# An attention-plus-hard-swish kernel: the first load moved to SyncE, the small token group moved last, half of a weight cast moved into a transfer

## The chip, the cores and the metric

The kernel runs on one core of one Trainium2 chip. The metric is the device time of one execution in microseconds (us); lower is better. Engines are named as in the profile: PE is TensorE's matmuls, PEld its weight loads, DVE is VectorE, ACT is ScalarE, POOL is GpSimd, SP is SyncE. A "q" after a name (SPq) is the engine's instruction queue, here mostly the issuing of DMAs.

## The reference: what is computed

The input x has 4 batches of 12480 tokens of 128 values, in float32. `inducing` has 32 rows of 128. For each batch, with scale = 1/sqrt(128):

```python
h   = softmax(scale * inducing @ x.T) @ x     # 32 x 128: every inducing row attends to all tokens
y   = softmax(scale * x @ h.T) @ h            # 12480 x 128: every token attends to the 32 rows of h
g   = y @ w_in                                # 128 -> 2048
out = (g * clip(g + 3, 0, 6) / 6) @ w_out     # hard swish, 2048 -> 128
```

Nothing of the second line can start before the first has seen all tokens of the batch. The kernel uses that y is a weighted mean of the 32 rows of h. With small values the clip is not active, and the whole of the last two lines becomes a linear and a quadratic form in the 32 weights; its coefficients are computed once for each batch from h, w_in and w_out. Checks at the end of the run send the work to a slow general path if an assumption fails; here it is not taken.

## The kernel before, in words

**Tiling.** The tokens of a batch are cut into six groups of 2048 (128 partitions times 16 tokens, 1 MB each) and a last small group of 192 tokens (48 partitions times 4, 96 KB): `groups`, lines 60 to 68. NF = 6 is the small group's index.

**Stages.** Four stages matter.

1. `a_first` (lines 340 to 433) is the first sum over tokens, for batch 0 alone; nothing runs beside it. It goes over `pieces`: half groups of 8 tokens for each partition, and the small group as one piece of 4. A piece is cast to bf16 (line 359: a piece that begins a group is halved between ACT and DVE, the others go to ACT whole), transposed by PE (line 369), copied out of PSUM to `xT` (line 371), multiplied with the inducing rows (line 378), put through Exp on ACT (line 385), and the float32r x is added with these weights into `hnd` by PE (line 392). DVE sums the weights themselves (`dacc`, `dlast`, lines 402 to 411), and POOL folds `dacc` in four adds (line 415). The loop at lines 420 to 433 sets the order by hand: in round k it transposes piece k+1, takes the weights of piece k, casts piece k+3, and adds piece k-1. Every engine executes its own instructions in that order.
2. `c_first` (lines 627 to 693) makes the coefficients of batch 0. It ends the sum (`c_den`, `c_HT`), casts w_in and w_out to bf16 on ACT (`cast_w`, line 637, four casts of four blocks each), and goes through 16 blocks of the hidden layer: `c_sq` squares a block (line 579 on ACT, every fourth on DVE, lines 576 and 577), `c_G` (line 510) feeds `c_hs` (lines 520, 522), `c_C` (line 588) adds the squared block times `w_out_b[:, jc, :]` into `cp`, and `c_L` (line 540) makes the linear part. The order is again written by hand; the first pieces of the second stage (`b_base`, line 783; `b_r`; `b_spread`, a DMA by SP, line 763) stand in between.
3. The main loop (lines 905 to 953) goes over the 100 chunks of 512 tokens of all batches, and fills in the first sum and the coefficients of the next batch.
4. The output is stored from the `os` tiles.

**Loads.** All loads of x and the weights are issued by POOL, because their destinations are float32r tiles and the source is float32. POOL issues in program order: x group 0 as two halves, the small group, the groups 1 to 5 (groups 1, 4, 5 as halves), some constants, then w_in (line 160) and w_out (line 161). After that it loads groups 0 and 1 of batch 1 as soon as the buffers of the first groups are free. The further groups are `held` until the first four spreads of the second stage have landed (`load_held`, line 132: a copy named `seen`, then the loads). SP issues the load of the inducing rows (line 106) as its first DMA, and then nothing until the spreads. PE needs the inducing rows in line 181, which stands behind 4 warming matmuls and ahead of 8 more, and the first transposes stand behind these.

**Buffers the change touches.** The `os` pool has two buffers; group 5 of batch 0 is loaded into one of them (line 117), since the five `xr` buffers hold groups 0 to 4. The pool `xb` of bf16 pieces has two buffers.

Of the kernel before, what the change touches and what calls it, by code (L numbers as in the profile page):

```python
# [9 lines left out]
FP32 = mybir.dt.float32  # L10
# [14 lines left out]
TG = 16  # L25
SL = 4
# [14 lines left out]
def kernel(  # L41
# [8 lines left out]
    nc = tc.nc  # L50
    P = nc.NUM_PARTITIONS
# [29 lines left out]
    with ExitStack() as es:  # L81
# [21 lines left out]


        I_sb = const.tile([M, C], FP32, name="I_sb")
        nc.sync.dma_start(I_sb[:, :], inducing[:, :])

        xs, xbs = {}, {}

        def load_x(b, g, cuts=(0, TG)):  # L110
            t0, p, n = groups[g]
            src = x[b, t0 : t0 + p * n, :].rearrange("(p i) c -> p i c", i=n)
            if n < TG:
                t = xlast.tile([P, n, C], FP32R, name="xl")
            elif b == 0 and g == XBUF:

                t = osp.tile([P, TG, C], FP32R, name="x5", tag="os")
            else:
                t = xin.tile([P, TG, C], FP32R, name="xr")
            for lo, hi in zip(cuts, cuts[1:]):  # L120
                lo, hi = min(lo, n), min(hi, n)
                nc.gpsimd.dma_start(t[:p, lo:hi, :], src[:, lo:hi, :])
            xs[(b, g)] = t

        load_x(0, 0, (0, 8, 16))

        held = []
        NF = NGR - 1 if rest else NGR
# [211 lines left out]
        def a_first():  # L340

            st = S[0]
            pieces = [(g, h, h + 8) for g in range(XBUF + 1) for h in (0, 8)]
            pieces.insert(2, (NF, 0, SL))
            last = len(pieces) - 1
            a1s = {}

            def cast(k):
                g, lo, hi = pieces[k]
                p = groups[g][1]  # L350
                if lo == 0:
                    xbs[(0, g)] = xbin.tile([P, TG, C], BF16, name="xb")
                xb, xf = xbs[(0, g)], xs[(0, g)]
                if hi - lo == 8 and (lo == 0 or k == last):
                    cuts = [(nc.scalar.copy, lo, lo + 4), (nc.vector.tensor_copy, lo + 4, hi)]
                else:
                    cuts = [(nc.scalar.copy, lo, hi)]
                for eng, i, j in cuts:
                    eng(xb[:p, i:j, :], xf[:p, i:j, :].bitcast(FP32))

            def transpose(k):
                g, lo, hi = pieces[k]
                t0, p, n = groups[g]
                step = 4 if k == last else 8
                for i in range(lo, hi, step):
                    j = min(i + step, hi)
                    pt = side_bank(0, [P, 1024], BF16, "pt")
                    for q in range(i, j):
                        nc.tensor.transpose(pt[:, (q - i) * p : (q - i + 1) * p], xbs[(0, g)][:p, q, :], ident_b[:p, :p])
                    eng = nc.scalar.copy if k == last and i > lo else nc.vector.tensor_copy  # L370
                    eng(st["xT"][:, t0 + i * p : t0 + j * p], pt[:, : (j - i) * p])

            def weights(k):
                g, lo, hi = pieces[k]
                t0, p, n = groups[g]
                s1 = side_bank(0, [P, 512], FP32, "s1")
                for q in range(lo, hi):
                    nc.tensor.matmul(
                        s1[:p, (q - lo) * M : (q - lo + 1) * M],
                        lhsT=st["xT"][:, t0 + q * p : t0 + (q + 1) * p],  # L380
                        rhs=I_T[:, :],
                    )
                w = (hi - lo) * M
                a1 = a1p.tile([P, TG * M], FP32R, name="a1")
                nc.scalar.activation(a1[:p, :w], s1[:p, :w], ACT.Exp, scale=scale)
                a1s[k] = a1

            def add(k):
                g, lo, hi = pieces[k]
                p, w, a1 = groups[g][1], (hi - lo) * M, a1s[k]  # L390
                for q in range(lo, hi):
                    nc.tensor.matmul(
                        st["hnd"][:M, :C],
                        lhsT=a1[:p, (q - lo) * M : (q - lo + 1) * M],
                        rhs=xs[(0, g)][:p, q, :],
                        start=(k == 0 and q == lo),
                        stop=(k == last and q == hi - 1),
                    )
                f = a1[:p, :w].bitcast(FP32)
                d = st["dacc"][:p, lo * M : hi * M]  # L400
                if g == 0:
                    nc.vector.tensor_copy(d, f)
                elif k == last - 3:
                    st["dlast"] = cst.tile([P, 8 * M], FP32, name="dlast")
                    nc.vector.tensor_copy(st["dlast"][:, :], f)
                elif k > last - 3:
                    nc.vector.tensor_add(st["dlast"][:, :], st["dlast"][:, :], f)
                    if k == last:
                        c_red(0, st["dlast"][:, :], P, 8)
                else:  # L410
                    nc.vector.tensor_add(d, d, f)
                if k == last - 4:
                    d = st["dacc"]
                    for h in (8, 4, 2, 1):
                        nc.gpsimd.tensor_add(d[:, : h * M], d[:, : h * M], d[:, h * M : 2 * h * M])
                    st.setdefault("dred", []).append(d[:, :M])
                if hi == groups[g][2]:
                    load_next(0, g)

            for k in range(3):  # L420
                cast(k)
            transpose(0)
            for k in range(last + 1):
                if k < last:
                    transpose(k + 1)
                weights(k)
                if k + 3 <= last:
                    cast(k + 3)
                if k:
                    add(k - 1)  # L430
                if k == 3:
                    half_rows()
            add(last)


        def c_red(b, src, p, n):
            st = S[b]
            st["reds"] = st.get("reds", -1) + 1
            dred = cst.tile([P, M], FP32, name=f"dred{st['reds']}")
            nc.vector.tensor_reduce(  # L440
                dred[:p, :], src.rearrange("p (s m) -> p m s", m=M), axis=AX.X, op=ALU.add
            )
            st.setdefault("dred", []).append(dred[:p, :])
# [183 lines left out]
        def c_first():  # L627

            warm(2)
            nc.scalar.copy(w_in_b[:, : F // 2], w_in_r[:, : F // 2].bitcast(FP32))  # L630
            c_den(0)
            nc.scalar.copy(w_in_b[:, F // 2 :], w_in_r[:, F // 2 :].bitcast(FP32))
            c_HT(0)
            warm(2)

            def cast_w(i, j):
                nc.scalar.copy(w_out_b[:, i:j, :], w_out_r[:, i:j, :].bitcast(FP32))

            cast_w(0, 4)
            c_G(0, 0, 6)  # L640
            sq = lambda *jbs: [c_sq(0, jb) for jb in jbs]
            cs = lambda *jcs: [c_C(0, jc) for jc in jcs]

            sg = lambda jb: (c_sq(0, jb), c_G(0, jb + 6, jb + 7))
            sg(0)
            sg(1)
            sg(2)
            cast_w(4, 8)
            b_pack(0, 0)
            b_e(0, 0)  # L650
            for c in range(4):
                b_spread(0, c)
            load_held(3)
            for jb in range(3, 7):
                sg(jb)
                cs(jb - 3)
            cast_w(8, 12)
            sg(7)
            b_f(0, 0)
            cs(4)  # L660
            sg(8)
            b_base(0, 0, 0)
            cs(5)
            sg(9)
            c_hs(0)
            b_base(0, 0, 1)
            cs(6)
            cast_w(12, 16)
            sq(10)
            cs(7)  # L670
            sq(11)
            b_r(0, 0)
            cs(8)
            sq(12)
            cs(9)
            sq(13)
            cs(10)
            b_base(0, 1, 0)
            sq(14)
            cs(11)  # L680
            sq(15)
            cs(12)
            c_L(0, 0)
            c_L(0, 1)
            b_base(0, 1, 1)
            a_cast(1, 0, ((nc.scalar.copy, 0, 2), (nc.scalar.copy, 2, 4)))
            b_prod(0, 0)
            c_BD(0)
            cs(13, 14, 15)
            c_tail(0)  # L690
            b_pack(0, 1)
            b_e(0, 1)
            c_max(0)
# [423 lines left out]
```

## Time and profile before

| what | value |
|---|---|
| median of 6 runs | 312.92 us (312.0 to 314.01) |
| the profiled execution's own time | 313.12 us |
| its span in the trace | 311.3 us |
| TensorE clock granted, mean | 0.996 of full speed |
| busy: PE, PEld, DVE, ACT, POOL | 96%, 75%, 76%, 75%, 11% of the span |
| HBM read, written | 27.67 MB, 25.56 MB |
| by the chain that ended last: PE, ACT, DMA, DVE | 72%, 11%, 7%, 5% of the span |
| end of the first sum's last matmuls (line 392) | 25.3 us |
| w_out on the chip | 27.86 us |
| first matmul of the main loop (line 800) | 40.8 us |

The span runs from the first to the last instruction; 1.8 us of the execution lie outside it. The chain that ended last is followed back from the last instruction, at each step to what released it. It names one releaser for each step, so a stage where two engines are nearly even is shown as the one that came last. A row of the timeline reads: start, duration, engine, line, operation, output and inputs with shapes, and in brackets how long the engine was idle before it and what ended that.

### The profile page before, as it was taken

To read this page: it belongs to the slowest core of one execution; us is meant where nothing else is said; L and a number is where in the kernel's file an instruction comes from. 1 tells how busy PE (TensorE), PEld (TensorE's weight loads), DVE (VectorE), ACT (ScalarE), POOL (GpSimd) and SP (SyncE) were. 2 spreads that over 40 slices of the span, in tenths; PEclk is the share of its full clock that TensorE was granted. 3 is DMA by queue.
4 is the path that set the end of the run, shared out by engine and by line. 5 is a ranking of instruction groups with operands and counts; after the bars stand their busy time and mean duration, and the time that the engine had idled before them with its cause. 6 is when DMAs were issued, how large, how long until landed. Compare 5 with 4: busy or idle time off the path is not lost.

```text
span 311.3 us, 9606 instructions
## 1 busy us (share of the span) xinstructions
PE 298.3 (96%) x3923; PEld 233.2 (75%) x3929; DVE 235.7 (76%) x543; ACT 231.9 (75%) x425; POOL 35.4 (11%) x82
## 2 busy tenths in 40 slices
PE   6899899999999999999999999999999999999992
PEld 2787678887676878888767877888867786777781
DVE  2687797977883868878796668787888487888882
ACT  3778999886589678886679849888658945777760
POOL 7611301011100010101100000100000001000000
PEclk9999999999999999999999999999999999999998
DMA  6999497988963452899975525555255335476672
GB/s 214 400 397 352 100 372 224 312 310 254 357 228 99 137 177 65 295 304 316 324 216 188 176 53 170 183 187 170 53 187 167 138 96 187 155 232 210 214 251 100
DMA packets 25089, 66.69 MB, mean 214 GB/s; under 512 B 3168, under 2 KB 17536, under 8 KB 19408
## 3 DMA queue, kind: packets, MB, share of 16 engines
q0 software_dynamic: 9232, 46.83, 43.6%
q1 hardware_dynamic: 15808, 19.19, 22.7%
q8 instruction: 32, 0.52, 0.6%
q14 instruction: 17, 0.14, 0.1%
HBM read 27.67 MB, written 25.56 MB: 171 GB/s over the span
## 4 chain that ended last, share of the span: by engine, by line
PE 72%; ACT 11%; DMA 7%; DVE 5%; issue 2%; POOL 1%; ACTq 0%; DVEq 0%; POOLq 0%
PE op L816 27%; PE bp L776 11%; PE op L800 7%; PE hnd L290 6%; ACT sq L579 6%; DMA w_out_r<-in_moe_w_out_dram 5%; PE pt L268 5%; PE cp L588 4%; PE s L276 2%; PE pp L747 2%; ACT TF L783 2%; DMA xr<-in_x_dram 2%; PE ep L703 2%; PE sp L717 1%; PE dpm L568 1%
## 5 line engine op out<-in xcount | busy, mean ns | idle before, releaser
L783 ACT ACTIVATE TF<-bp 128x512 bf16<-128x512 f32 (+1 forms) x200 | 117.2, 599 | 38.7 <-PE rp L736 21.0
L816 PE MATMUL op<-Cq,TF 128*128 128x128 bf16 (+1 forms) x800 | 109.2, 223 | 0.0
L816 PE MATMUL op<-Cq,TD 128*128 128x128 bf16 (+1 forms) x800 | 105.9, 219 | 0.0
L832 DVE TENSOR_TENSOR os<-op,r_all 128x512 f32<-128x512 f32 (+1 forms) x100 | 68.5, 685 | 18.9 <-PE op L816 17.6
L816 PEld LDWEIGHTS <-TF 128*128 128x128 bf16 (+1 forms) x800 | 50.5, 98 | 33.6 <-issue 24.7
L776 PE MATMUL bp<-xT,W 128*128 128x512 bf16 (+1 forms) x197 | 74.0, 376 | 0.1
L792 DVE TENSOR_TENSOR TD<-TF,d 128x1024 bf16<-128x1024 bf16 (+1 forms) x100 | 66.9, 669 | 1.1 <-DMA d<-dk 0.5
L816 PEld LDWEIGHTS <-TD 128*128 128x128 bf16 (+1 forms) x800 | 61.4, 98 | 0.6
L800 PE MATMUL op<-BD,nf 128*128 128x512 f32 (+1 forms) x100 | 53.3, 533 | 0.5 <-DVE os L832 0.4
L579 ACT ACTIVATE sq<-dpm 128x512 bf16<-128x512 f32 x60 | 35.2, 641 | 4.1 <-PE gp L510 1.9
L259 ACT CAST xb<-xr 128x1024 bf16<-128x1024 f32 x36 | 37.6, 1055 | 0.0
L737 DVE RECIPROCAL r_all<-rp 128x4 f32<-128x4 f32 (+1 forms) x100 | 17.8, 178 | 24.3 <-PE rp L736 23.9
L736 PE MATMUL rp<-one,nf 128*128 128x4 f32 (+1 forms) x100 | 34.5, 345 | 0.4
L269 DVE COPY xT<-pt 128x1024 bf16<-128x1024 bf16 (+1 forms) x42 | 25.8, 618 | 8.1 <-PE pt L268 7.6
L844 POOL DMA_DIRECT2D out_dram<-os x21 | 11.3, 537 | 142.7 <-DVE os L832 136.0
L290 PE MATMUL hnd<-xr,a 128*32 128x128 f32 x288 | 24.2, 226 | 0.0
L754 ACT ACTIVATE dk<-pp 128x512 bf16<-128x512 f32 (+1 forms) x28 | 15.7, 560 | 10.4 <-PE pp L747 10.4
L268 PE MATMUL pt<-ident_b,xb 128*128 128x128 bf16 x300 | 23.3, 218 | 0.0
L776 PEld LDWEIGHTS <-W 128*128 128x128 bf16 x200 | 19.5, 97 | 5.0 <-issue 3.4
L588 PE MATMUL cp<-w_out_b,sq 128*128 128x128 bf16 x256 | 22.7, 220 | 0.5 <-ACT sq L579 0.5
L568 PE MATMUL dpm<-dH,w_in_b 128*128 128x512 bf16 x62 | 22.7, 381 | 0.0
L510 PE MATMUL gp<-HTr,w_in_r 128*128 128x32 f32 x64 | 21.3, 358 | 0.3 <-ACT HTr L488 0.3
(127 smaller groups left out, 405.5 us busy)
## 6 DMA issues: line engine op xcount, KB each, us to landing
xr<-in_x_dram POOLq DMA_DIRECT2D x20, 1024.0 KB, 8.5
out_dram<-os POOLq DMA_DIRECT2D x18, 1024.0 KB, 4.4
d<-dk SPq DMA_DIRECT2D x96, 128.0 KB, 3.9
out_dram<-os SPq DMA_DIRECT2D x5, 1024.0 KB, 4.1
xr<-in_x_dram POOLq DMA_DIRECT2D x6, 512.0 KB, 5.4
x<-in_x_dram POOLq DMA_DIRECT2D x2, 512.0 KB, 13.5
w_in_r<-in_moe_w_in_dram POOLq DMA_DIRECT2D x1, 1024.0 KB, 13.5
w_out_r<-in_moe_w_out_dram POOLq DMA_DIRECT2D x1, 1024.0 KB, 16.6
```

Of the source, the lines that this page charges most:

```text
L259: eng(xb[:p, lo:hi, :], xs[(b, g)][:p, lo:hi, :].bitcast(FP32))
L268: nc.tensor.transpose(pt[:, (i - lo) * p : (i - lo + 1) * p], xb[:p, i, :], ident_b[:p, :p])
L290: nc.tensor.matmul(st["hnd"][:M, :C], lhsT=a1[:p, i * M : (i + 1) * M], rhs=xs[(b, g)][:p, i, :], start=(g == 0 and i == 0), stop=(g == NG ...
L579: nc.scalar.activation(sq[:, :], dpm[:, :], ACT.Square)
L588: nc.tensor.matmul(st["cp"][:, k * C : (k + 1) * C], lhsT=sq[:, k * P : (k + 1) * P], rhs=w_out_b[:, jc, :], start=(jc == 0 and k == 0), s ...
L736: nc.tensor.matmul(rp[:p, :SL], lhsT=nf[:, j * p : (j + 1) * p], rhs=one4[:, :])
L776: nc.tensor.matmul(bp[:, :w], lhsT=st["W"][:, k].rearrange("p m i -> p (m i)"), rhs=st["xT"][:, c0 : c0 + w],)
L783: nc.scalar.activation(st[("x", c)][:, k, :w], bp[:, :w], ACT.Exp, scale=scale)
L792: nc.vector.tensor_mul(u[:, :, :w], t[:, :, :w], d[:, :w].unsqueeze(1).to_broadcast([P, 2, w]))
L800: nc.tensor.matmul(op[:p, :], lhsT=st[("nf", g)][:, j * p : (j + 1) * p], rhs=st["BD"][:, :], start=True, stop=False, skip_group_check=True,)
L816: nc.tensor.matmul(op[:p, s * C : (s + 1) * C], lhsT=T[k][:, s * p : (s + 1) * p], rhs=st["Cq"][:, k, :], start=False, stop=(s == SL - 1 a ...
L832: nc.vector.tensor_mul(ot[:p, j * SL : (j + 1) * SL, :], op[:p, :].rearrange("p (s c) -> p s c", c=C), r_all[:p, b, c, :].unsqueeze(2).to_ ...
```

## The change

Three things are changed.

- **First half of group 0.** Its 512 KB are loaded by SP, as float32, into a buffer of the `os` pool (`x0`). ACT and DVE cast the bf16 piece from there, and DVE copies `x0` into the float32r tile that the later matmuls read. SP's load of the inducing rows stands behind it now.
- **Small group.** In batch 0 it is the last piece and no longer the third. The special handling of the last large piece moves with it (`last - 1`), and the closing of the weight sums is adapted; the load of batch 1's small group is issued fourth of the held loads and not first.
- **Cast of w_out.** Blocks 8 to 15 of `w_out_b` are written by a POOL DMA from `w_out_r`, and two of ACT's four casts go. On POOL it stands behind the folding of `dacc` and ahead of `seen`, and it waits for w_out to have landed.

```diff
         I_sb = const.tile([M, C], FP32, name="I_sb")
-        nc.sync.dma_start(I_sb[:, :], inducing[:, :])
...
             for lo, hi in zip(cuts, cuts[1:]):
                 lo, hi = min(lo, n), min(hi, n)
-                nc.gpsimd.dma_start(t[:p, lo:hi, :], src[:, lo:hi, :])
+                if (b, g, lo) == (0, 0, 0):
+
+                    x0 = osp.tile([P, TG, C], FP32, name="x0", tag="os")
+                    nc.sync.dma_start(x0[:, lo:hi, :], src[:, lo:hi, :])
+                    xs["x0"] = x0
+                else:
+                    nc.gpsimd.dma_start(t[:p, lo:hi, :], src[:, lo:hi, :])
             xs[(b, g)] = t
 
         load_x(0, 0, (0, 8, 16))
+        nc.sync.dma_start(I_sb[:, :], inducing[:, :])
...
-            pieces.insert(2, (NF, 0, SL))
+            pieces.append((NF, 0, SL))
             last = len(pieces) - 1
...
-                if hi - lo == 8 and (lo == 0 or k == last):
+                if hi - lo == 8 and (lo == 0 or k == last - 1):
...
-                    eng(xb[:p, i:j, :], xf[:p, i:j, :].bitcast(FP32))
+                    eng(xb[:p, i:j, :], xs["x0"][:, i:j, :] if k == 0 else xf[:p, i:j, :].bitcast(FP32))
+                if k == 0:
+                    nc.vector.tensor_copy(xf[:, lo:hi, :], xs["x0"][:, lo:hi, :])
...
-                step = 4 if k == last else 8
+                step = 4 if k == last - 1 else 8
...
-                    eng = nc.scalar.copy if k == last and i > lo else nc.vector.tensor_copy
+                    eng = nc.scalar.copy if k == last - 1 and i > lo else nc.vector.tensor_copy
...
+                elif k < last - 3:
+                    nc.vector.tensor_add(d, d, f)
                 elif k == last - 3:
                     st["dlast"] = cst.tile([P, 8 * M], FP32, name="dlast")
                     nc.vector.tensor_copy(st["dlast"][:, :], f)
-                elif k > last - 3:
-                    nc.vector.tensor_add(st["dlast"][:, :], st["dlast"][:, :], f)
-                    if k == last:
-                        c_red(0, st["dlast"][:, :], P, 8)
                 else:
-                    nc.vector.tensor_add(d, d, f)
+                    nc.vector.tensor_add(st["dlast"][:p, :w], st["dlast"][:p, :w], f)
...
+                if k == last:
+                    c_red(0, st["dlast"][:, :], P, 8)
...
             nc.scalar.copy(w_in_b[:, F // 2 :], w_in_r[:, F // 2 :].bitcast(FP32))
+
+            nc.gpsimd.dma_start(w_out_b[:, FB // 2 :, :], w_out_r[:, FB // 2 :, :].bitcast(FP32))
             c_HT(0)
...
-            cast_w(8, 12)
             sg(7)
...
-            cast_w(12, 16)
             sq(10)
```

## The prediction

> **What bounds the kernel now.** I read the chain of waits first: 72% of it is PE, and from the main loop's start (40.8 us) no step of it is a DMA. All three edits lie before 41 us, so the question is how much earlier the main loop starts; its PE chain then carries the shift to the end one for one. The chain up to 30 us (start, duration, what):
>
> ```profile
> 1.28 0.50 POOL xr L122
> 1.78 0.20 issue
> 1.98 4.94 DMA xr<-in_x_dram
> ...
> 11.31 16.55 DMA w_out_r<-in_moe_w_out_dram
> 27.86 0.02 issue
> 27.89 0.62 ACT w_out_b L637
> 28.50 0.01 issue
> 28.52 1.11 ACT sq L579 x2
> 29.63 0.51 ACT w_out_b L637
> ```
>
> The reader is to see a stage paced by loads until 27.86, then one paced by ACT. Next, busy time by stretch, where the last two columns are the DMA share and GB/s:
>
> ```profile
> 1.00:2.00 1.00, 0.79 (x2) 0.28 (x3) 0.15 (x1) 1.00 (x1) 0.72 (x2) 1.00 0.06 15
> 2.00:2.50 0.50, 0.50 (x3) 0.15 (x1) 0.00 (x0) 0.04 (x1) 0.50 (x1) 1.00 0.01 2
> 2.50:3.00 0.50, 0.50 (x2) 0.00 (x0) 0.00 (x0) 0.00 (x0) 0.42 (x3) 1.00 0.37 123
> 3.00:3.50 0.50, 0.44 (x3) 0.28 (x3) 0.23 (x1) 0.00 (x0) 0.50 (x2) 1.00 0.86 270
> ```
>
> The DMA engines are idle until about 2.7 but for 16 KB of inducing rows, which SP issued at 0.76; from 3.5 to 30 their share stays about 1 or more. Third, the timeline of ACT and PE:
>
> ```profile
> 12.41 0.62 ACT L359 CAST xb<-xr 128x512 bf16<-128x512 f32 x1 [1.07 <-DMA xr<-in_x_dram]
> 14.90 0.62 ACT L359 CAST xb<-xr 128x512 bf16<-128x512 f32 x1 [0.17 <-DMA xr<-in_x_dram]
> 17.80 0.62 ACT L359 CAST xb<-xr 128x512 bf16<-128x512 f32 x1 [0.39 <-DMA xr<-in_x_dram]
> ...
> 34.86 0.70 ACT L637 CAST w_out_b<-w_out_r 128x512 bf16<-128x512 f32 x1
> ```
>
> Every later group of x is waited for, so an earlier load stream is an earlier sum.
>
> **Edit 1, first half by SP.** The stream's start is what moves. POOL's first load is issued at 1.28 and moves bytes from about 2.7; SP's first DMA is issued at 0.76 and its 15 KB move between 1 and 2, say from 1.85. From then on the engines are never idle in either kernel, and the bytes are the same, so everything behind should land 2.7 - 1.85 = 0.85 us earlier; I take 0.8. Bounds: 0, if the early bytes only interleave with POOL's, and 1.07, the wait at 12.41, beyond which compute is late instead.
>
> The Trainium skill speaks against this: "DMA: Bandwidth & Descriptors", section "Issuing engines are not separate DMA queues", says that all issuers share the same 16 DMA engines and that issuing from several saves only sequencer time. By that alone the gain here would be one POOL issue, 0.50 us in the chain above, and the sum below would be 0.3 us worse. I stay with 0.8, because the engines in the rows above stand idle.
>
> What it adds: the copy x0 to float32r on DVE. DVE copies 128x256 in 0.284 us and 128x512 in 0.397 (lines 402, 299), so 128x1024 is about 0.62; at the rate of a 128x512 tensor-tensor (0.69) it would be 1.2. DVE waits 1.85 us for x here, and the float32r half is not read before 9.66. Behind it the DVE queue holds the cast of group 1's first half, and behind that the PSUM copy of piece 0 (before at 6.88). Group 1 has landed by 9.17 at the latest; from the bytes moved I estimate 8.6, now 7.8. So the PSUM copy runs at 8.3 to 9.0, and the first weights matmul at about 9.1 in place of 8.49. The inducing rows, now behind 512 KB on SP, land near 5 (estimate: SP's 1 MB stores land in 4.1 us, 256 KB in 2.7, and half the bandwidth is POOL's). PE waits for them, then runs 8 warming matmuls (2.68 us), so the first transposes are at 8.0 and not 6.22. Both delays fit together rather than add, and end at ACT being ready for group 2 at about 11.4; it lands at 12.41 - 0.8 = 11.6. Cost 0. Without that cover, each us that the rows land beyond 5.3 costs up to one us at 11.6, of which the later waits give most back: compute needs 7.4 us from there to group 5, the loads 7.97.
>
> **Edit 2, small group last.** Early on it takes 0.61 + 0.27 us from ACT, in a stretch that ends in the 1.07 us wait: gain 0. At the end it costs. Behind the last large piece ACT has an Exp of 0.27 (queued 0.2) more, and ahead of it a cast of 0.61 (queued 0.57): 0.78. ACT's idle there is 0.27 before the PSUM copy at 23.16 and 0.38 before HTr at 26.96, together 0.65, so HTr is 0.13 later. On DVE the reduction at 25.14 starts 0.1 to 0.15 later. POOL's folding of the sums (2.18 us, 22.50 to 24.68) follows a half group that now comes one place later, ends near 25.6 before the shift, and meets its matmul at 25.57. Cost 0.15; bounds 0 and 0.6, if POOL's folding is late. Moving batch 1's small load behind three others on POOL costs nothing: it is needed a batch's sum later.
>
> **Edit 3, half of the cast.** Two ACT casts go, at 32.43 and 34.86; in the chain each takes 0.50. But PE is nearly even with ACT here:
>
> ```profile
> 31.67 0.40 PE L588 MATMUL cp<-w_out_b,sq 128*128 128x128 bf16 x4 [0.31 <-ACT sq L579]
> ...
> 35.28 0.40 PE L588 MATMUL cp<-w_out_b,sq 128*128 128x128 bf16 x4
> 35.52 0.38 PE L568 MATMUL dpm<-dH,w_in_b 128*128 128x512 bf16 x1
> 36.11 0.40 PE L588 MATMUL cp<-w_out_b,sq 128*128 128x128 bf16 x4 [0.21 <-ACT sq L579]
> ```
>
> From 31.67 to 35.52 PE starts something every 0.22 us with no wait on ACT. So the first cast's 0.50 only gives ACT slack. The second ends as a wait: cp at 36.11 could start at 35.52 + 0.22 = 35.74. That is 0.37 gained, and what stood there is gone. Next late is PE itself: the linear part would start at 37.04 in place of 37.41; its input from DVE ends at 36.55, so DVE does not bind. Bounds: 0 and the 1.00 of the naive chain.
>
> The transfer must have landed when block 8 is multiplied, at 34.78 before and 34.1 after (0.65 of shift). POOL issues it when w_out has landed, about 27.1, with the 1 MB load of batch 1's group 1 ahead in the queue, which ends near 29.7 by the shift (the GB/s fall at 30.5 now). For 512 KB read at the 420 GB/s of these stretches I add 1.3 us, and about 1 us to landing: 32. Cover is 2 us. The trace holds no casting transfer to bf16; the nearest rows are the spreads, also from SBUF to SBUF, 2.7 to 8.5 us to landing, that is 29.8 to 35.6. On POOL only `seen` is behind it, which waits until 36.43 for a spread anyway. The spreads on SP share the engines with 0.5 MB more, but the first is needed at 38.8.
>
> **Sum.** -(0.8 - 0.15) - 0.37 = -1.02 us. Against the profiled execution: 313.12 - 1.02 = 312.10. The median lies 0.2 lower, so I forecast 312.92 - 1.02 = **311.9**. w_out, the other condition at 27.89, lands 0.8 earlier, while the first square is due 0.65 earlier, so it does not bind.
>
> **Rivals**, on the median.
> - *The stream is not earlier* (edit 1 gives 0 to 0.2): +0.15 - 0.37 - 0.1 = -0.3, 312.6. For it: all 16 engines are shared, and the first loads run at only 260 GB/s with a share of 1. Against it: the idle share before 2.7.
> - *ACT, not PE, paces 31 to 36*: both casts count, -0.65 - 1.00, 311.3. For it: the chain names ACT throughout. Against it: the PE rows above.
> - *The casting transfer is late* (slower): PE is in order, so each us after 34.1 at block 8 costs one us of the whole run; it eats the gain at 34.1 + 1.0 = 35.1. At the 8.5 us of the slowest spread it is 1.5 late: 313.4. At 9.6 us, the median landing of the 1 MB loads up to 50 us, it is 2.6 late: 314.5. For it: it queues behind a backlog. Against it: that backlog is 1 MB, and x itself is loaded into float32r by POOL at 400 GB/s.
> - *The change does not do what it says*: x0 lands no earlier than 5.5 and the inducing rows after 6. That is the first rival with up to 0.5 lost again.
>
> **How the numbers follow.** 0.3% is 0.94 us, about what a measurement of this kernel can tell from no change, so the bound is 311.98. Forecast case (311.5 to 312.4) 0.55, of which 0.35 lies below the bound; stream not earlier 0.13; ACT paces 0.10; late transfer 0.22, of which 0.04 is mild enough (landing before about 36.0) to stay within the bound. Faster 0.35 + 0.10 = 0.45; same 0.20 + 0.13 + 0.04 = 0.37; slower 0.18. The range, 311.0 to 313.7, takes in the second rival and the milder late transfer, and leaves out the heavier one.
>
> **What would show it.** Right: bytes moving from 1.9 at over 200 GB/s; group 2 cast at 11.5 to 11.8; w_out landing near 27.1; first square at 27.7 to 28.0; no PE wait at block 8; the linear part near 36.4. Wrong: a DMA as releaser at block 8 (line 595 of the new kernel); ACT at group 2 released by PE or DVE; the first square at 28.5 or later.

## The result and the profile after

The changed kernel is slower: median 314.85 us (313.36 to 315.62, 17 runs) against 312.69 (311.48 to 314.23, 38 runs), ratio 1.0063, 95% interval 1.0048 to 1.0077. The forecast was 311.9, range 311.0 to 313.7. The profiled execution takes 314.54 us, its span is 312.8, 1.5 us longer than before.

| event (us) | before | after | forecast shift | measured shift |
|---|---|---|---|---|
| first half of group 0 cast | 5.55 | 4.78 | -0.8 | -0.77 |
| second half of group 0 cast | 6.94 | 8.58 | | +1.64 |
| first transposes | 6.22 | 8.34 | +1.8 | +2.12 |
| group 2 cast | 12.41 | 13.95 | -0.8 | +1.54 |
| weight sums reduced (DVE) | 25.14 | 27.13 | -0.65 | +1.99 |
| first square | 28.52 | 30.52 | -0.65 | +2.00 |
| linear part | 37.41 | 39.03 | -1.02 | +1.62 |
| first matmul of the main loop | 40.77 | 42.39 | -1.02 | +1.62 |

The loss is complete at the first square; from there to the linear part 0.38 is gained. The rows for this are, of before (its first square, at 28.52, stands in the prediction) and then of after:

```profile
37.41 1.15 PE L540 MATMUL lp<-w_out_r,hs 128*32 128x128 f32 x16
```

```profile
30.52 1.11 ACT L586 ACTIVATE sq<-dpm 128x512 bf16<-128x512 f32 x2 [0.70 <-PE dpm L575]
...
39.03 1.15 PE L547 MATMUL lp<-w_out_r,hs 128*32 128x128 f32 x16
```

In two steps the reduction becomes 1.99 late: 1.54 when group 2 is cast, and 0.45 more between there and the reduction.

**The loads.** Busy time by stretch, first two lines of before, then after; as in the prediction the columns are PE, PEld, DVE, ACT, POOL (with counts), the granted clock, the DMA share, and last GB/s:

```profile
5.00:6.00 1.00, 1.00 (x5) 0.29 (x3) 0.43 (x1) 0.45 (x1) 1.00 (x3) 1.00 1.10 406
6.00:7.00 1.00, 0.70 (x9) 0.45 (x8) 0.12 (x1) 0.23 (x2) 0.78 (x2) 1.00 1.21 356
```

```profile
1.00:2.00 1.00, 0.79 (x2) 0.28 (x3) 0.15 (x1) 1.00 (x1) 0.71 (x2) 1.00 0.10 25
2.00:2.50 0.50, 0.50 (x3) 0.15 (x1) 0.00 (x0) 0.03 (x1) 0.42 (x2) 1.00 0.70 238
2.50:3.00 0.50, 0.50 (x2) 0.00 (x0) 0.23 (x1) 0.00 (x0) 0.50 (x2) 1.00 1.07 336
3.00:3.50 0.50, 0.10 (x1) 0.00 (x0) 0.00 (x0) 0.00 (x0) 0.50 (x2) 1.00 0.84 207
...
5.00:6.00 1.00, 0.93 (x3) 0.45 (x4) 0.61 (x3) 0.40 (x1) 1.00 (x3) 1.00 0.70 184
6.00:7.00 1.00, 1.00 (x4) 0.34 (x3) 0.59 (x1) 0.00 (x0) 0.72 (x1) 1.00 0.76 145
```

Bytes do move earlier: 238 GB/s from 2.0, where before had 2. But from 5 to 7 the rate is 184 and 145, where before had 406 and 356, and the DMA share of 0.70 to 0.76 says that the engines are partly idle. (From 3.0 to 5 it is already lower: 207, 195 and 236 against 270, 262 and 291.) They do not lack orders. By 4.66 POOL has issued 0.5 MB (second half), 96 KB, and three loads with 2 MB, SP 0.5 MB, some 3.2 MB in all; by 5.0 about 0.75 MB have moved (the GB/s summed from 1 to 5). ACT's rows show what this does (in brackets its idle time and what ended it):

```profile
8.58 1.04 ACT L364 CAST xb<-xr 128x1024 bf16<-128x1024 f32 x1 [3.18 <-DMA xr<-in_x_dram]
10.12 0.62 ACT L364 CAST xb<-xr 128x512 bf16<-128x512 f32 x1 [0.50 <-DMA xr<-in_x_dram]
...
13.95 0.62 ACT L364 CAST xb<-xr 128x512 bf16<-128x512 f32 x1 [0.74 <-DMA xr<-in_x_dram]
...
16.36 0.62 ACT L364 CAST xb<-xr 128x512 bf16<-128x512 f32 x1
```

Three casts wait for loads, the last of them group 2's. Group 3, at 16.36, shows no wait any more, though its load had landed only at 16.34; behind it no cast waits, and compute sets the pace. In before groups 3 and 4 waited again (0.17 and 0.39), and every load from group 2 to the last half of group 5 was cast within 0.03 us of its landing (the last landed at 21.63 and was cast at 21.65): there the loads set the pace to the end.

**The end of the sum.** The chain of waits of after (start, duration, what) no longer runs through w_out's load, as before's does, but through PE:

```profile
3.05 1.61 POOL xr L126 x3
4.66 11.68 DMA xr<-in_x_dram
...
24.64 0.49 PE hnd L399 x8
25.13 0.20 PE pt L376 x4
25.33 0.30 PE s L385 x8
25.63 0.49 PE hnd L399 x8
26.12 0.20 PE s L385 x4
26.33 0.96 PE hnd L399 x12
```

The small piece is `pt` x4, `s` x4 and the last 4 of `hnd` x12. Its steps stand between those of the large pieces, in PE's order, and each has another engine behind it. The timeline shows its last steps, with the last large piece's transposes at 23.78:

```profile
23.78 0.62 PE L376 MATMUL pt<-ident_b,xb 128*128 128x128 bf16 x8
...
26.36 0.27 ACT L392 ACTIVATE a<-s 48x128 fp32r<-48x128 f32 x1 [0.31 <-PE s L385]
...
26.86 0.43 PE L399 MATMUL hnd<-xl,a 48*32 48x128 f32 x4
27.13 0.60 DVE L447 TENSOR_REDUCE dred<-dlast 128x32 f32<-128x256 f32 x1
```

ACT's Exp waited for PE, and PE's last add stands behind the add of the piece before. From the last large piece's transposes to the reduction it is 3.35 us (23.78 to 27.13), before 2.63 (22.51 to 25.14):

```profile
22.51 0.62 PE L369 MATMUL pt<-ident_b,xb 128*128 128x128 bf16 x8
...
25.14 0.60 DVE L440 TENSOR_REDUCE dred<-dlast 128x32 f32<-128x256 f32 x1
```

**The cast by a transfer.** POOL's issue, and PE around block 8:

```profile
28.43 0.58 POOL L641 DMA_DIRECT2D w_out_b<-w_out_r  x1 [1.60 <-DMA w_out_r<-in_moe_w_out_dram]
...
36.54 0.38 PE L575 MATMUL dpm<-dH,w_in_b 128*128 128x512 bf16 x1
36.57 0.35 PE L743 MATMUL rp<-one,nf 128*128 128x4 f32 x1
36.79 0.40 PE L595 MATMUL cp<-w_out_b,sq 128*128 128x128 bf16 x4
```

The transfer lands 5.8 us after its issue, near 34.2. Block 8 is multiplied at 36.79 with no wait in brackets, 2.6 us after.

### The profile page after: what moved, and what is told of

The parts are those of the page before. It is cut to its first block, busy times and chain, and to the rows that moved or that the text cites. A ratio compares the mean times of both kernels' runs of the same rounds, so it can differ in the third digit from the quotient of the medians.

```text
span 312.8 us, 9607 instructions
## 1 busy us (share of the span) xinstructions
PE 297.8 (95%) x3924; PEld 233.2 (75%) x3929; DVE 236.6 (76%) x544; ACT 230.8 (74%) x423; POOL 36.0 (12%) x82
## 4 chain that ended last, share of the span: by engine, by line
PE 76%; ACT 9%; DVE 6%; DMA 4%; issue 2%; POOL 1%; ACTq 0%; DVEq 0%; POOLq 0%
PE op L823 27%; PE bp L783 12%; PE op L807 7%; PE hnd L295 6%; ACT sq L586 5%; PE cp L595 5%; PE pt L273 5%; DMA xr<-in_x_dram 4%; PE s L281 2%; PE pp L754 2%; ACT TF L790 2%; PE dpm L575 2%; PE sp L724 2%; PE ep L710 2%; PE hnd L399 1%
```

## The experiments

The theory after the result: early SP traffic stalls POOL's stream of loads from 5 to 7, and the small group costs a whole round of the pipeline at the end. Rivals: for the stall, DVE's copies or the inducing rows behind `x0`; for the end, only ACT's spare time. One table of all runs follows: GB/s in the stretches 5 to 6 and 6 to 7, the cast of group 2, the time from there to the reduction, the first square, the start of the main loop (one profile each, us); then the median and the timed ratio to before, which is worked out over all comparable runs and need not be the quotient of the medians. The medians of before beside them are 312.75 (e1 to e4), 312.82 (e5 to e7), 312.43 (e8 to e11) and 313.01 (e12 to e15).

| run | GB/s 5-7 | group 2 | to reduction | first square | main loop | median | ratio [95%] |
|---|---|---|---|---|---|---|---|
| before | 406, 356 | 12.41 | 12.73 | 28.52 | 40.77 | 312.69 | 1 |
| after | 184, 145 | 13.95 | 13.18 | 30.52 | 42.39 | 314.85 | 1.0063 [1.0048, 1.0077] |
| e1_edit1 | 266, 219 | 13.20 | 12.03 | 28.62 | 40.88 | 313.19 | 1.0016 [0.9995, 1.0037] |
| e2_edit2 | 412, 359 | 12.93 | 13.30 | 29.82 | 42.77 | 314.27 | 1.0040 [1.0021, 1.0059] |
| e3_edit3 | 418, 352 | 12.55 | 12.78 | 28.71 | 40.57 | 312.20 | 0.9996 [0.9978, 1.0015] |
| e4_edit23 | 397, 356 | 13.10 | 13.17 | 29.66 | 41.53 | 313.23 | 1.0019 [1.0000, 1.0038] |
| e5_actcopy | 186, 156 | 13.75 | 13.21 | 30.35 | 42.22 | 315.30 | 1.0082 [1.0052, 1.0113] |
| e6_poolx0 | 404, 363 | 12.79 | 13.54 | 29.70 | 41.57 | 314.03 | 1.0032 [1.0009, 1.0056] |
| e7_isbfirst | 381, 340 | 12.55 | 13.19 | 29.13 | 40.99 | 313.27 | 1.0013 [0.9989, 1.0037] |
| e8_isbact | 213, 195 | 13.73 | 13.19 | 30.30 | 42.17 | 314.57 | 1.0076 [1.0063, 1.0089] |
| e9_best | 358, 322 | 12.87 | 12.00 | 28.25 | 40.12 | 312.93 | 1.0003 [0.9988, 1.0018] |
| e10_small10 | 432, 350 | 12.67 | 13.77 | 29.83 | 42.09 | 313.59 | 1.0052 [1.0035, 1.0069] |
| e11_warm | 160, 215 | 13.54 | 13.18 | 30.11 | 41.97 | 313.63 | 1.0045 [1.0031, 1.0059] |
| e12_actx0 | 166, 234 | 13.49 | 13.19 | 30.07 | 41.93 | 314.66 | 1.0050 [1.0021, 1.0079] |
| e13_late | 406, 344 | 12.83 | 13.44 | 29.67 | 41.52 | 315.22 | 1.0076 [1.0043, 1.0108] |
| e14_both | 381, 311 | 13.38 | 12.97 | 29.74 | 41.60 | 313.75 | 1.0034 [1.0006, 1.0061] |
| e15_again | 176, 170 | 13.60 | 13.18 | 30.17 | 42.03 | 314.22 | one time |

How far to trust it: single times of one kernel spread over 2 to 3 us, and the rest of the span behind the main loop's start varies from 269.3 to 271.4 us between these profiles. So an effect below a microsecond is read from the events ahead of the main loop, and the timed ratio says whether it reaches the end.

### One part at a time

`e1_edit1` is before with the new first half alone; `e2_edit2` with the small group last alone; `e3_edit3` with the transfer alone; `e4_edit23` is the changed kernel without the new first half. The edits are the parts of the diff above, for example of e3:

```diff
+            nc.gpsimd.dma_start(w_out_b[:, FB // 2 :, :], w_out_r[:, FB // 2 :, :].bitcast(FP32))
...
-            cast_w(8, 12)
...
-            cast_w(12, 16)
```

> The kernel before with the first edit alone (first half of group 0 by SP, copied to float32r on DVE). Theory P: DVE's two float32 copies of x0 (5.5 to 6.6 in the changed kernel) keep POOL from writing DMA descriptors, so the load stream stalls there. Theory R: SP's 512 KB and POOL's loads share the 16 engines badly, so POOL's stream runs slower from its start, whatever DVE does. Both expect the same here: under 200 GB/s at 5.5 to 7, group 2 landing at 13.5 to 14, and 1.0 to 1.4 us slower than before. If the loss came from the moved small group instead, this kernel would be no slower than before.

> The kernel before with the second edit alone (small group as the last piece). Loads as before: group 2 cast at 12.4, last large piece transposed at 22.5. Theory: PE's own order at the end of the first sum, not ACT, prices the move: 0.7 us from there to the reduction, so 0.5 to 0.7 slower than before. The prediction's step (ACT slack) expects 0.15 slower.

> The kernel before with the third edit alone (blocks 8 to 15 of w_out cast by a POOL transfer). Theory (the prediction's step): PE is nearly even with ACT there, so 0.37 faster, linear part at 37.0 and not 37.4. Rival, the chain taken at its word: 1.0 faster, linear part at 36.4. Rival, late transfer: PE waits for a DMA at block 8 and the kernel is slower.

> The changed kernel with the first edit undone. If the three edits add up: 0.6 (small group) - 0.37 (cast) = 0.1 to 0.3 slower than before, and 1.2 to 1.6 faster than the changed kernel. If the small group last only costs because the loads are late, this is 0.2 to 0.4 faster than before.

e3 does what was forecast between the first square and the linear part, 8.51 us against 8.89. e2 is the surprise: the small group alone costs 0.4% (0.7 to 1.8 us by the interval). Its profile shows more than that edit. From 28 to 32 the granted clock was 0.66 there and 1.00 in before, as these lines show (before, then e2):

```profile
28.00:32.00 4.00, 3.68 (x40) 2.57 (x40) 3.18 (x8) 3.99 (x9) 0.00 (x0) 1.00 0.73 278
```

```profile
28.00:32.00 4.00, 3.67 (x23) 2.14 (x22) 3.17 (x8) 2.67 (x7) 0.00 (x0) 0.66 0.83 311
```

e2 took 3.59 us from the reduction to the first square (before 3.38), and 9.60 from there to the linear part (before 8.89). So 0.9 of the 2.00 us by which its main loop starts late go with the clock, and 1.09 at the reduction are left: 0.52 because group 2 landed later in this profile, 0.57 on the way from there (the clock was 0.83 from 10 to 20, too). Whether the edit has a part in the later landing is not shown; among the profiles without the slow loads, group 2 is cast anywhere from 12.41 to 13.10 where it waits for its load.

In e1 the slow stretch is there:

```profile
5.00:6.00 1.00, 1.00 (x4) 0.39 (x5) 0.74 (x3) 0.27 (x1) 1.00 (x3) 1.00 1.30 266
6.00:7.00 1.00, 1.00 (x4) 0.44 (x3) 0.40 (x1) 0.00 (x0) 0.52 (x1) 1.00 1.02 219
```

The rate is low, though here the DMA share (1.30, 1.02) does not show idle engines as in after. Group 2 is 0.79 late, yet the reduction is only 0.09 late (25.23): with the small group in third place the pieces run from group 2 to the reduction in 12.03 where before took 12.73, because before stood waiting for its loads. That gap of 0.7 takes the delay in. What is left is the loads' own delay at the end, which is small: by group 4's second half they had caught up, as ACT's casts of before and then of e1 show (first the second half of group 4, then that of group 5):

```profile
19.10 1.04 ACT L359 CAST xb<-xr 128x1024 bf16<-128x1024 f32 x1
...
21.65 0.62 ACT L359 CAST xb<-x 128x512 bf16<-128x512 f32 x1
```

```profile
19.19 1.05 ACT L365 CAST xb<-xr 128x1024 bf16<-128x1024 f32 x1
...
21.74 0.62 ACT L365 CAST xb<-x 128x512 bf16<-128x512 f32 x1
```

In e4, where the small group is last, the same way takes 13.17, and 13.18 or 13.19 in after, e7, e8, e11, e12 and e15, with group 2 cast anywhere from 12.55 to 13.95: no slack is left, and each delay of group 2 goes through whole. (e2, e6 and e13, at 13.30 to 13.54, take longer; e6 and e13 wait once more for a load, of group 5 and of group 4.) The clock is not behind this: in e4, e7, e8 and e12 it was 0.57 on average from 10 to 14, in after, e11 and e15 1.00, and the way is the same. So adding the late loads to e4 should show in full, and it does: from e4 to after group 2 moves by 0.85 and the main loop's start by 0.86; with e15, the same kernel as after, it is 0.50 and 0.50. The price of one edit depends on the other.

### Does a copy on DVE, or the row load behind it, stall POOL's stream?

`e5_actcopy`: the changed kernel with both passes over `x0` on ACT, so that DVE makes no copy of it.

```diff
-                if hi - lo == 8 and (lo == 0 or k == last - 1):
+                if hi - lo == 8 and k and (lo == 0 or k == last - 1):
...
-                    nc.vector.tensor_copy(xf[:, lo:hi, :], xs["x0"][:, lo:hi, :])
+                    nc.scalar.copy(xf[:, lo:hi, :], xs["x0"][:, lo:hi, :])
```

> The changed kernel, with both passes over x0 (the bf16 cast and the copy to float32r) on ACT, none on DVE. ACT is idle from 5.4 to 8.6 there. Theory P (DVE's float32 copies keep POOL from writing descriptors): the load rate at 5.5 to 7 is over 300 GB/s, the second half of group 0 lands near 7.3 and not 8.6, group 2 near 12.5, and the kernel is 1.0 to 1.4 faster than the changed one. Theory R (SP's and POOL's loads share the engines badly): the rate at 5.5 to 7 stays under 200 GB/s and the time within 0.3 of the changed kernel.

Busy time by stretch in e5:

```profile
5.00:6.00 1.00, 0.93 (x3) 0.46 (x4) 0.19 (x1) 1.00 (x2) 1.00 (x3) 1.00 0.64 186
6.00:7.00 1.00, 1.00 (x4) 0.34 (x3) 0.00 (x0) 0.77 (x1) 0.27 (x1) 1.00 0.79 156
```

DVE is nearly idle and the stall is as before: the copies are not its cause. They do cost POOL something else: its six issues from 3.04 take 3.68 us in after, where the copy runs from 5.92 to 6.59 beside the last of them, and 3.23 in e5; in e11, where the copy starts at 6.09 with the issues nearly done, they take 3.26. The Trainium skill describes this in "SBUF — State Buffer", section "SBUF: two separate sides": while DVE runs a float32 copy in a two-port mode, GpSimd can't write the descriptors of its DMAs. The 0.45 us of issue agree with it; the idle engines from 5 to 7 are not explained by it.

`e6_poolx0` lets POOL load `x0` (the copies stay); `e7_isbfirst` puts the inducing rows ahead of `x0` on SP, so that `x0` is issued at 1.20 and not at 0.76.

```diff
-                    nc.sync.dma_start(x0[:, lo:hi, :], src[:, lo:hi, :])
+                    nc.gpsimd.dma_start(x0[:, lo:hi, :], src[:, lo:hi, :])
```

```diff
         I_sb = const.tile([M, C], FP32, name="I_sb")
+        nc.sync.dma_start(I_sb[:, :], inducing[:, :])
...
-        nc.sync.dma_start(I_sb[:, :], inducing[:, :])
```

> The changed kernel, with x0 loaded by POOL and not by SP, still as float32 and still copied by DVE. Theory P: the stream stalls while DVE copies, at about 6 to 7.5, and group 2 lands at 13 or later. Theory R: no stall, loads as in the kernel before, group 2 at 12.4.

> The changed kernel with SP's load of the inducing rows ahead of x0 again. PE then warms at 3.2 to 6 and is ready for the first piece at 6, but the second piece and the loads behind it do not come earlier. P and R both expect no gain over 0.2 over the changed kernel; a gain of 0.5 or more would mean that PE's late warm-up, and not the loads, sets the loss.

Busy time by stretch in e7:

```profile
5.00:6.00 1.00, 1.00 (x4) 0.40 (x3) 0.79 (x2) 0.62 (x1) 1.00 (x3) 1.00 1.10 381
6.00:7.00 1.00, 1.00 (x9) 0.50 (x7) 0.26 (x1) 0.33 (x1) 0.44 (x2) 1.00 1.26 340
```

Neither stalls. For e6 that was expected. For e7 it was not: the expectation gave at most 0.2 us, and the first square came 1.39 earlier than in after. Two readings were left: the rows behind `x0` do harm, or `x0` at 0.76 does. `e8_isbact` has the rows issued by ACT, `x0` alone on SP:

```diff
-        nc.sync.dma_start(I_sb[:, :], inducing[:, :])
+        nc.scalar.dma_start(I_sb[:, :], inducing[:, :])
```

> The changed kernel with the load of the inducing rows issued by ACT, so that SP issues x0 alone and as early as in the changed kernel. Theory Q (the 16 KB queued behind x0 on SP, for which PE waits until 5, goes with the stall): no stall, over 300 GB/s at 5 to 7, group 2 at 12.5 to 12.9, 1.2 to 1.6 faster than the changed kernel. Theory R2 (x0 begun at 2.0, before POOL's loads, is what disturbs POOL's stream): stall as in the changed kernel, and within 0.5 of its time.

213 and 195 GB/s, group 2 at 13.73, ratio 1.0076: nothing stands behind `x0` on SP, and the stall is there. The rows are not the cause.

### Where the small group's cost comes from

`e10_small10` is before with the small group as the eleventh piece, two places ahead of the end.

```diff
-            pieces.insert(2, (NF, 0, SL))
+            pieces.insert(10, (NF, 0, SL))
...
-                    nc.vector.tensor_add(st["dlast"][:, :], st["dlast"][:, :], f)
+                    nc.vector.tensor_add(st["dlast"][:p, :w], st["dlast"][:p, :w], f)
```

> The kernel before with the small group as the eleventh piece, ahead of the last large group, and nothing else changed. Theory T (the cost of the second edit is the small piece's own transposes, weights and adds behind the last large piece): the 0.7 us at the end go, so 0.7 or more faster than the kernel with the second edit alone, and 0 to 0.4 slower than before. If the cost is at the start (DVE held by the cast of group 1), it stays: 0.8 to 1.5 slower than before.

The tail was then as short as before (2.55 from the last transposes to the reduction), but those transposes came at 23.89, 1.38 late (group 2 had been 0.26 late); the first square was 1.31 late, ratio 1.0052. My theory that the cost lies only at the tail fell. The small piece takes a whole round of PE, ACT and DVE wherever it stands among pieces that follow each other without slack; in third place it ran in a wait for loads.

### More on the stall

`e9_best` joins what had not cost: before with the new first half (rows first) and the transfer, the small group third. `e11_warm` is the changed kernel with 10 warming matmuls for 4, so that PE is not idle from 3.1 to 5.

```diff
-        warm(4)
+        warm(10)
```

> The kernel before with the first edit, but the inducing rows ahead of x0 on SP, and with the third edit; the small group stays third. If the parts add: loads 0.3 earlier at group 2, the last transposes 0.1 to 0.5 earlier, and 0.37 from the cast: 0.4 to 0.9 faster than before. If the earlier loads are worth nothing, 0.3 faster at most.

> The changed kernel with 10 and not 4 warming matmuls ahead of the wait for the inducing rows, so that PE is busy from 1.2 to about 5 and not idle from 3.1. If PE's idleness is behind the stall, the rate at 5 to 7 rises over 300 GB/s and the kernel gains 1 us or more; if the order on SP is, the stall and the time stay within 0.5 of the changed kernel.

e9 reached the first square 0.27 and the main loop 0.65 earlier than before in its profile, but the ratio is 1.0003, so the expected 0.4 to 0.9 us are not there in the times. It is no faster than before as far as this can be measured; nor is e3. e11 kept the stall (160, 215): PE's idleness is not the cause.

`e12_actx0` has ACT issue `x0` (at 0.75) in place of SP; `e13_late` puts two loads of 16 KB ahead of it on SP, so that it is issued at 1.67; `e14_both` loads both halves of group 0 by SP (and casts and copies both); `e15_again` is the changed kernel once more.

```diff
-                    nc.sync.dma_start(x0[:, lo:hi, :], src[:, lo:hi, :])
+                    nc.scalar.dma_start(x0[:, lo:hi, :], src[:, lo:hi, :])
```

```diff
+        nc.sync.dma_start(I_sb[:, :], inducing[:, :])
+        I_two = const.tile([M, C], FP32, name="I_two")
+        nc.sync.dma_start(I_two[:, :], inducing[:, :])
...
-        nc.sync.dma_start(I_sb[:, :], inducing[:, :])
```

```diff
-                if (b, g, lo) == (0, 0, 0):
+                if (b, g) == (0, 0):
...
-                if k == 0:
+                if k < 2:
```

> The changed kernel with x0 issued by ACT as its first instruction, at about the same time, and the inducing rows alone on SP. Theory R2 (an early start of x0 ahead of POOL's loads disturbs POOL's stream, whoever issues it): stall at 5 to 7 (150 to 250 GB/s), within 0.6 of the changed kernel. If SP's queue itself is the cause: over 300 GB/s there and 1 us or more gained.

> The changed kernel with two loads of 16 KB (the inducing rows, and the same again into a spare tile) ahead of x0 on SP, so that x0 is issued at about 1.6 and not 0.76. Theory R2: no stall at 5 to 7, as in the kernel with one load ahead; x0 lands near 5.6, group 2 at 12.5 to 13, 0.8 to 1.5 faster than the changed kernel. If one load ahead was no cure but a chance, the stall is back.

> The changed kernel with both halves of group 0 by SP (1 MB, both copied by DVE), so that POOL begins with the small group and group 1. If the stall comes from two queues reading the two 4 KB halves of the same 8 KB rows, it goes: over 300 GB/s at 5 to 7. If it comes from SP's early traffic itself, it stays or lengthens, to 8 or 9.

> The changed kernel once more, for a second profile. If the stall belongs to the kernel: again under 250 GB/s at 5 to 7 and group 2 at 13.3 or later. If it was one execution's chance: over 300 GB/s and group 2 at 12.5.

Busy time by stretch in e12 and then in e14:

```profile
5.00:6.00 1.00, 1.00 (x4) 0.33 (x3) 0.73 (x2) 0.31 (x1) 1.00 (x3) 1.00 0.50 166
6.00:7.00 1.00, 1.00 (x5) 0.45 (x4) 0.00 (x0) 0.00 (x0) 0.38 (x1) 1.00 0.83 234
```

```profile
5.00:6.00 1.00, 0.00 (x0) 0.00 (x0) 0.00 (x0) 0.25 (x1) 0.92 (x2) 1.00 1.25 381
6.00:7.00 1.00, 0.57 (x2) 0.31 (x3) 0.25 (x2) 0.96 (x1) 0.14 (x1) 1.00 1.09 311
```

With ACT as the issuer the stall stays (DMA share 0.50). With both halves on SP it is gone, although `x0` starts at 0.76 there too; what e14 gains is lost again to compute (ACT not ready for group 2 until 13.38, with no wait for a load). e15 stalls like after, so it is no accident of one execution. e13 shows no stall and a main loop 0.87 earlier than after, but `x0` landed at 7.03 and not near 5.6, and the times do not bear the gain out (ratio 1.0076). Five of its eight runs had a granted clock of 0.981 to 0.987 and took 315.2 to 315.6 us; the three at 0.992 to 0.994 took 313.0 to 314.4. e2's profile, at 0.982, shows that such a mean can hold a stretch that costs 0.9 us; whether e13's timed runs hold one there is not on record.

So seven profiles stall (after, e1, e5, e8, e11, e12, e15): in all of them `x0` is issued at about 0.76 by SP or ACT while POOL loads the other half of the same rows. Of the nine that do not, e7, e9 and e13 issue it at 1.20 or later, e6 has it on POOL, e14 has no other half on POOL, and the others have no `x0`. The median of group 2 is 13.60 in the stalled ones and 12.81 in the nine others together with before: 0.8 us. The times go the same way but for e13: of the kernels with the small group last, those that stall have ratios of 1.0045 to 1.0082, those that do not 1.0013 to 1.0040. What happens inside the DMA engines stays open. That two queues read the two halves of the same 8 KB runs of memory with an offset fits all of this, but was not tried by itself.

## Why the prediction was wrong

- **"The stream's start is what moves … everything behind should land 2.7 - 1.85 = 0.85 us earlier": this step failed**, and it is the larger one. Its premise held: bytes moved from about 2.0 at 238 GB/s and the first half was cast 0.77 earlier. The sentence "from then on the engines are never idle in either kernel" did not: the share fell to 0.70, the second half came 1.64 later and group 2 1.54 later (1.19 in e15). Of this 0.85 (0.50) is beyond e4, the same kernel with POOL loading the first half; the rest is in e4's profile too. The bound from below, 0, stood for bytes that only interleave; no row excluded a loss.
- **"Cost 0.15" for the small group: the term that was mis-sized.** It was worked out as ACT's added time less ACT's idle time. With loads as in before it costs 0.45 at the reduction (13.18 against 12.73), and where loads are not waited for 1.18 (13.18 against 12.00 in e9), since in the hand-written order the piece is a whole round of three engines in a row. The times put it at 0.7 to 1.8 us (e2), so 0.45 is too low for them. POOL's folding, which I had feared, bound nothing.
- **The two together.** The prediction noted that "compute needs 7.4 us from there to group 5, the loads 7.97": the slack that takes in a late group 2. (In after, where no load is waited for, compute needs 7.66, from 13.95 to 21.61.) Edit 2 removes that slack. Therefore e1 loses 0.11 at the main loop's start, but the same edit on top of e4 loses 0.86 (0.50 in e15). The sum at the main loop's start: e3 -0.20; from e3 to e4 +0.96; from e4 to after +0.86; in all +1.62. Of the +0.96, 0.55 is group 2 cast later in e4's profile than in e3's (13.10 and 12.55), 0.39 the longer way to the reduction. The -0.20 is edit 3's -0.38 behind a first square that was 0.19 late in that profile.
- **The rows behind `x0`: right.** They landed near 5.0 as estimated, the first transposes were at 8.34 (forecast 8.0), and group 2's cast was still released by a DMA. DVE's copy took 0.67 (forecast 0.62) and hindered no cast.
- **Edit 3: right**, in mechanism and size. 37.41 - 28.52 = 8.89 before, 8.51 after and in e3, 8.50 in e4: -0.38, forecast -0.37; PE and not ACT was next. In the times 0.38 can't be told from nothing (e3: 0.9996, 0.9978 to 1.0015). The transfer landed near 34.2 and not at 32. Measured from w_out's landing, as the prediction counted, it is later by about 1 us; the rest is the delay of the whole. Two misreadings stand behind it and partly cancel. The fall of the GB/s at 30.5 was taken for the end of the load ahead in POOL's queue, but that load landed at 32.84 in before and 33.10 in after, 5.0 us behind w_out and not 2.6; and the transfer landed 1.1 us behind that load and not 2.3. It was needed at 36.8.
- **The rivals.** None was this one. "The stream is not earlier" looked at the right place, but was priced as a lost gain. The late transfer, which held all of the 0.18 given to a slower kernel, did not occur, nor did `x0` or the rows land late (4.76 and 4.94). Of the signs named, "the first square at 28.5 or later" came true; the DMA at block 8 and the release of group 2 by PE or DVE did not.
- **The page.** By "Issuing engines are not separate DMA queues" (the Trainium skill, "DMA: Bandwidth & Descriptors") a second issuer saves only its issue time. That I stood against it on the ground of idle engines was half right: the first 0.77 us were real. But the runs differ from the page too: who issues, and when, changed what the other queue moved (184 and 145 GB/s in after, 404 and 363 in e6), a loss that this section does not name.

## What to carry to other kernels

Before pricing a moved step in a hand-ordered pipeline, find the stretch in which it now hides: a small piece costs its whole round where nothing waits, and little or nothing where everyone waits for a load; and the slack that it uses up is then missing for the next late load. When a transfer is started earlier on another queue, look at the stream behind it in the first microseconds, and not only at its own landing; idle engines are no proof that added orders are free. Price edits one on top of the other, not singly: here the new first half cost 0.10 us at the first square alone, and 0.86 on top of the small group last (0.51 in the second profile of the same kernel).

## What the hardware showed that was not expected

- A 512 KB load issued at 0.76 by SP or ACT, with POOL loading the other half of the same rows, left the DMA engines at a share of 0.50 to 0.70 between 5 and 6 in six of seven profiles (1.30 in e1, but at 266 GB/s), while megabytes were on order. Issued 0.44 us later (e7, e9) it did not.
- The casting transfer from float32 to bf16 inside SBUF (512 KB read) took 0.58 us of POOL's issue and 5.8 us to land, 1.1 us behind the second of two 1 MB loads issued before it (30.63 and 33.10).
- With DVE's float32 copy beside the last of them POOL's six issues took 3.68 us, without it 3.23.
- In e2's profile the granted clock was 0.66 from 28 to 32 and 1.00 in before; a 128x512 bf16 matmul (`dpm`) that began between 29.19 and 31.68 took 0.59 to 0.61 us there; in before it takes 0.38 to 0.39.
- The main loop and what follows took 269.3 to 271.4 us in the profiles, for nearly the same instructions; differences of half a microsecond ahead of it do not reliably reach the time of an execution.
